# Windowed attention with a mixture of experts: all heads of q and k of six late groups loaded in 128 B runs by quarters of partitions and turned by VectorE, and the expert pieces of a step grouped two and two

## The chip, the cores and the metric

The kernel runs on one core of a Trainium2 chip. The metric is the device time of one execution in microseconds, the median of the runs. A core has TensorE (PE; its weight loads are shown as PEld), VectorE (DVE), ScalarE (ACT), GpSimd (POOL), and SyncE (SP), which here issues most transfers. Each engine works through its own instructions in a fixed order and waits on semaphores for the others; 16 DMA engines move the data.

## The reference

q, k and v are 8 batches × 8 heads × 576 positions × 64, all f32. Each position sees itself and the 63 before it. The attention's rows (4608 tokens of 512) then go through a layer of 8 experts, of which each token takes the one with the largest logit:

```python
rel = pos[:, None] - pos[None, :]
scores = np.where((rel >= 0) & (rel < 64), q @ k.T / 8, -1e9)
x = softmax(scores) @ v                      # heads side by side: (4608, 512)
logits = x @ w_gate + modality_bias[modality_id]
e = argmax(logits); gate = softmax(logits)[e]
out[rows of e] = gate * (relu(x[rows of e] @ w1[e]) @ w2[e])   # 512 -> 1024 -> 512
```

## The kernel before

**Attention.** The sequence is cut into 72 blocks of 64 positions, two blocks to a step `s` (36 steps, then four that drain), two steps to a group `G` of four blocks. Step `s` issues, in this order: `values` (the product with v) and `logits` for earlier steps, `scores(s)`, `minima(s)` on VectorE, `probs_t(s - 1)` (the probabilities turned by TensorE), `exps` on ScalarE, and `x_t(s - 2)`, the turning of the attention's finished rows, which logits of the next step reads. A step also prepares half of the next group's q and k: step 2G - 2 turns the heads of k of group G, step 2G - 1 those of q, in two parts of four heads each (`PARTS`). `heads_t` makes four TensorE transposes of 128 × 128 against an identity, two heads of even or odd positions in each; `heads_out` copies the result out of PSUM into `kT` or `qT` (VectorE; ScalarE for the second half of k). In the second step of a group `route2` ranks the tokens of an earlier group R by expert (three small matmuls, the "ranks"), `route3` and VectorE turn the ranks into addresses (`cnt`, `tgt`), and `scatter` writes the rows to a scratch in memory, sorted by expert.

**PSUM.** From step FIRST = 12 on, `turn_bank` gives the logits, the probabilities, the rows, the ranks and the q and k parts a bank each in turn out of a pool of two (`tp`). A part waits until the bank two turns back has been read.

**Experts.** From step 12 on the two most frequent experts already work, on slots of 256 rows out of the scratch. A slot is cut into 16 pieces of TensorE work of equal size (`first`: w1, lines L304; `second`: w2, L326; each product in three matmuls of high and low parts, so a hidden tile is split by ScalarE, `hh`, and VectorE, `hl`). `gap(it, True)` issues one piece; steps 12 and later have four such gaps, one behind the probabilities, one behind the rows, one behind each q or k part. Pieces that read hh and hl stand two pieces behind those that made them. When the attention is over, the rest of the slots run back to back.

**Loads.** `at` is a table from steps to loads, and a step issues its loads first, all on SP's queue: v of the step, k of group G in step 2G - 3 and q in step 2G - 2 (one step earlier for groups 1 to 7). Two `qk` buffers serve k and q in turns. SP also issues the weights (`y`, in `weights`) and the slots' rows (`xt`); it issues strictly in order, so one that waits holds up those behind it. Routing operations wait in a list (`routing`) that `tick` empties a few at a time; `run_later` issues what the last piece left for VectorE and ScalarE.

Of the kernel before, what the change touches and what calls it, by code (L numbers as in the profile page):

```python
# [8 lines left out]
F32 = mybir.dt.float32  # L9
# [17 lines left out]
def tile_window_attn_moe(  # L27
# [101 lines left out]
    def tick(n=1, table=False):  # L129
        for _ in range(n):  # L130
            if routing and not table:
                routing.pop(0)()
            elif queue:
                queue.pop(0)()
                issued[0] += 1
# [111 lines left out]
    def run_later():  # L247
        while later:
            later.pop(0)()
# [212 lines left out]
    def gap(it, wait=False):  # L462

        if next(it, "end") != "end" and not wait:
            run_later()
            tick()
# [40 lines left out]

    PARTS = ((K0, K1), (Q0, Q1))
    AHEAD = range(1, 8)
    WARM = 8, 3  # L510

    n_tp = [0]

    def turn_bank(s):

        i = n_tp[0]
        n_tp[0] += 1
        if s < FIRST and i % 5 > 1:
            return ps_m.tile([P, 512], F32, name=("em", "y0", "y1")[i % 5 - 2])
        return ps_t.tile([P, 512], F32, name="tp")  # L520
# [28 lines left out]
        else:  # L549
            qk[G, nm] = work.tile([P, 2, H, D], F32, name="qk", bufs=2)  # L550

    def load_qk(G, nm, blocks=range(GBLK), dma=nc.sync):

        t = qk[G, nm]
        x = q if nm == "q" else k
        i = blocks[0]
        while i <= blocks[-1]:
            b, g = divmod(GBLK * G + i, BPB)
            n = min(BPB - g, blocks[-1] + 1 - i)
            src = x[b, :, g * W64:(g + n) * W64].rearrange("h (p t) d -> p t h d", t=2)  # L560
            p0 = i * W64 // 2
            for par in range(2):
                dma.dma_start(out=t[p0:p0 + n * W64 // 2, par], in_=src[:, par])
            i += n

# [118 lines left out]
    def x_t(p, xp):  # L684
        xa = st[p, "xa"]
        for c in range(NC1):
            turn(xp[:, c * P:(c + 1) * P], xa[:, c * P:(c + 1) * P])
        xaT = st[p, "xT"] = work.tile([P, DM], F32, name="xaT")
        nc.scalar.copy(out=xaT, in_=xp)
# [13 lines left out]
            out=st[G, "lg"][:, j, :], in0=lt[:, 0:E], in1=bias_sel[:, p, :], op=ALU.add)  # L703

    chosen = {0: first_oh}

    def route1(G):

# [40 lines left out]
    def route3(G, rk):  # L749

        ex, oh = st.pop((G, "r")), chosen.pop(G)
        xg = [st.pop((GB * G + j, "xa")) for j in range(GB)]
        tgt = small.tile(sh3, F32, name="tgt")
        nc.vector.tensor_tensor(
            out=tgt, in0=rk.rearrange("p (j e) -> p j e", e=E), in1=ebase, op=ALU.add)
        se = small.tile([P, GB], F32, name="se")
        dst = small.tile([P, GB], F32, name="dst")
        idx = small.tile([P, GB], I32, name="idx")
        routing.append(lambda: nc.vector.reduce_sum(out=se, in_=ex, axis=AX.X))
        routing.append(lambda: nc.vector.tensor_tensor(out=tgt, in0=tgt, in1=oh[:, 1:], op=ALU.mult))  # L760
        routing.append(lambda: nc.vector.tensor_scalar(
            out=se, in0=se, scalar1=1e-9, scalar2=None, op0=ALU.add))
        routing.append(lambda: nc.vector.reduce_sum(out=dst, in_=tgt, axis=AX.X))

        def gates():
            for j in range(GB):
                nc.vector.reciprocal(out=xg[j][:, DM:DM + 1], in_=se[:, j:j + 1])
        routing.append(gates)

        def scatter(j):  # L770
            p = GB * G + j
            nc.gpsimd.tensor_copy(out=xg[j][:, DM + 1:DM + 2], in_=idc[:, p:p + 1])
            ins = nc.gpsimd.indirect_dma_start(  # L773
                out=xs, out_offset=bass.IndirectOffsetOnAxis(ap=idx[:, j:j + 1], axis=0),
                in_=xg[j], in_offset=None)
            tc.declare_no_dep(ins.ins, group="scatter", reason="rows are distinct")
            tc.add_to_no_dep_group("scatter", ins.ins)
            late = [T for T, _ in EARLY if T < G]
            if late:
                tc.declare_no_dep(ins.ins, group="early_loads", reason="rows read are older")  # L780
            for T in late:
                tc.add_to_no_dep_group(f"scatter_after_{T}", ins.ins)

        def rows():
            nc.vector.tensor_copy(out=idx, in_=dst)
            for j in range(GB):
                scatter(j)
            scattered.append(f"scatter_after_{G}")
        routing.append(rows)

    def counts(G, tp):
        cp = tp[:, GB * E:E + GB * E]
# [55 lines left out]
    def when(step, f, *args):  # L848
        at.setdefault(max(step, -1), []).append((f, args))
# [9 lines left out]
    for G in range(1, NG):  # L859
        ahead = 1 if G in AHEAD else 0  # L860
        for nm, step in (("k", 2 * G - 3 - ahead), ("q", 2 * G - 2 - ahead)):
            when(step, new_qk, G, nm)
            when(step, load_qk, G, nm)

    pieces = []
    raws = []
# [155 lines left out]

    for s in range(NPR + 4):
        j = s % GB
        for f, args in at.pop(s, ()):
            f(*args)
        n_tick = 6 if s < FIRST else 5
        n_gap = 0 if s < FIRST else 4
        G = s // GB + 1
        heads = PARTS[j] if G < NG else ()  # L1030
        R = (s - 5) // GB if s >= 5 and j == 1 else -1
        if 1 <= s < FIRST:
            swap_upper(s - 1)

        if 2 <= s < NPR + 2:
            values(s - 2)
            if s <= FIRST:
                values_out(s - 2)
        if 3 <= s < NPR + 3:
            logits(s - 3, turn_bank(s) if s != FIRST else ps_m.tile([P, 512], F32, name="y0"))  # L1040
            if (s - 3) % GB == GB - 1:
                route1((s - 3) // GB)
        if FIRST < s < NPR + 2:
            values_out(s - 2)
        if s < NPR:
            scores(s)
            if s == FIRST:
                x_turn(fetched[0])
                gap(it, True)
            minima(s)  # L1050
            if s == FIRST - 2:
                tick(todo[0][-1] - issued[0], table=True)
        if 1 <= s <= NPR:
            if s == FIRST:
                run_later()
            if s >= FIRST:
                swap_upper(s - 1)
            swap_v(s - 1)
            for a in range(2):
                probs_t(s - 1, a, turn_bank(s))  # L1060
            sums(s - 1)
        if s < NPR:
            exps(s, (0, 1))
        if s == 0:
            first_pair(1, (both[:1], both[1:]))
            cast_bias()
        if n_gap > 0 and s != FIRST:
            gap(it, True)
        if 2 <= s < NPR + 2:
            x_t(s - 2, turn_bank(s) if s != FIRST else ps_m.tile([P, 512], F32, name="y0"))  # L1070
        run_later()
        tick(2)
        if s < NPR:
            exps(s, (2, 3, 4))
        if n_gap > 0:
            if FIRST < s < FIRST + 4 or s % 2:
                weights(s)
            if s != FIRST:
                gap(it, True)
        if heads:  # L1080
            tp = turn_bank(s)
            heads_t(G, *heads[0], tp)
            heads_out(tp, G, *heads[0], nc.vector.tensor_copy)
        if s == FIRST:
            weights(s)
            gap(it, True)
        run_later()
        tick(n_tick)
        cnt = None
        if R >= 0:  # L1090
            tp = turn_bank(s)
            rk = route2(R, tp)
            if R == NG - 1 or any(R == T for T, _ in EARLY):
                cnt = counts_out(tab if R == NG - 1 else pl, counts(R, tp))
            route3(R, rk)
        if s < NPR:
            exps(s, (5, 6, 7))
        if n_gap > 2:
            if FIRST <= s < FIRST + 4:
                weights(s)  # L1100
            gap(it, True)
        if heads:
            tp = turn_bank(s)
            heads_t(G, *heads[1], tp)
            heads_out(tp, G, *heads[1], nc.scalar.copy if heads[1] == K1 else nc.vector.tensor_copy)
        run_later()
        tick(n_tick)
        if s == WEIGHTS:
            load_weights()
        if s >= WEIGHTS:  # L1110
            weights(s)
        if n_gap > 3:
            gap(it, True)
        run_later()
        if s == 1:
            select_bias()
        if s == 4:
            nc.sync.dma_start(out=xs_blk[DUMMY:DUMMY + 2].rearrange("b p c -> p b c"), in_=padrow)
        for T, xs_ in EARLY:
            if T == R:  # L1120
                plan(T, xs_, cnt)
    tick(len(routing))
    tick(len(queue))


# [266 lines left out]
```

## Time and profile before

| | |
|---|---|
| median of the runs | 622.13 us (621.25 to 622.3, three runs) |
| the profiled execution | 621.29 us, of which the program's span is 619.6 us |
| TensorE busy | 603.5 us |
| VectorE, ScalarE, GpSimd busy | 381.8, 297.4, 139.7 us |
| moved by DMA | 88.08 MB in 158983 packets |

Engine times are the union of an engine's instructions. TensorE's matmuls overlap one another, so the duration of one says less than the distance from its start to the start of the next. "Idle before" is time in which an engine stood still, with what ended it. Lines L are those of the kernel before.

### The profile page before, as it was taken

Reading aid. Unit: us, or ns where it says so; the run is one execution under the profiler, and the core shown is the slowest. Engines: PE = TensorE matmul, PEld = TensorE weight load, DVE = VectorE, ACT = ScalarE, POOL = GpSimd, SP = SyncE. Lnnn points to the kernel's source line nnn. Section 1 sums busy time; section 2 is a strip of 40 time slices with the busy share of each in tenths; the row PEclk is TensorE's granted clock in tenths of the full one; section 3 lists DMA queues with packets and bytes.
Section 4 is the critical chain, followed back from the end, with each engine's and each line's share of the span. In section 5 each row is a group of like instructions: output and inputs, shape, how many; then the busy total and the mean of one; then the engine's idle time right before and its main releaser. Section 6 shows DMA issues by size and latency. Waiting matters only on the chain. (4 is left out here: it accounts for less than half of the span.)

```text
span 619.6 us, 17314 instructions
## 1 busy us (share of the span) xinstructions
PE 603.5 (97%) x6365; PEld 542.2 (88%) x6365; DVE 381.8 (62%) x1486; ACT 297.4 (48%) x933; POOL 139.7 (23%) x315
## 2 busy tenths in 40 slices
PE   8999889999999999999999999999999999999996
PEld 5888778889898998989898899999999989999986
DVE  3899987877776877667656465323324734776622
ACT  3999886765757555636463111111112513554411
POOL 6333422042313320321223131011001101102202
PEclk7999999999999999999999999999999999999999
DMA  9999865764675754463313034522243534678300
GB/s 163 216 234 246 204 183 166 188 188 126 167 205 123 194 135 99 137 155 84 107 54 103 35 103 167 174 69 69 51 155 116 167 126 137 203 239 249 108 18 21
DMA packets 158983, 88.08 MB, mean 142 GB/s; under 512 B 122618, under 2 KB 141616, under 8 KB 158768
## 3 DMA queue, kind: packets, MB, share of 16 engines
q1 hardware_dynamic: 150272, 67.45, 43.1%
q0 software_dynamic: 5888, 18.93, 8.1%
q8 instruction: 51, 0.84, 0.6%
q10 hardware_dynamic: 2736, 0.58, 0.5%
q14 instruction: 36, 0.29, 0.2%
HBM read 67.49 MB, written 23.91 MB: 148 GB/s over the span
## 5 line engine op out<-in xcount | busy, mean ns | idle before, releaser
L326 PE MATMUL y<-Whi,hh 128*128 128x512 f32 x288 | 116.9, 406 | 0.0
L638 ACT ACTIVATE ss<-ss,mn 128x128 f32<-128x128 f32 x288 | 112.6, 398 | 4.0 <-DMA wg<-in_moe_w_gate_dram 3.3
L326 PE MATMUL y<-Wlo,hh 128*128 128x512 f32 x288 | 112.7, 391 | 0.0
L326 PE MATMUL y<-Whi,hl 128*128 128x512 f32 x288 | 112.5, 391 | 0.0
L337 POOL DMA_INDIRECT out_dram<-y,id x36 | 39.8, 1107 | 232.7 <-DVE y L334 159.9
L313 DVE SCALAR_TENSOR_TENSOR hl<-em,hh 128x512 fp32r<-128x512 f32 x50 | 34.5, 690 | 92.8 <-ACT hh L312 82.1
L304 PE MATMUL em<-xh,Whi 128*128 128x256 f32 x400 | 83.7, 290 | 0.0
L312 ACT ACTIVATE hh<-em 128x512 fp32r<-128x512 f32 x50 | 29.6, 592 | 105.2 <-PE em L304 86.9
L304 PE MATMUL em<-xl,Whi 128*128 128x256 f32 x400 | 79.3, 280 | 0.0
L304 PE MATMUL em<-xh,Wlo 128*128 128x256 f32 x400 | 79.1, 279 | 0.0
L647 ACT COPY pT<-tp 128x512 f32<-128x512 f32 x57 | 31.4, 589 | 70.2 <-PE tp L470 60.9
L626 DVE CUSTOM_DVE_ANT_0 ss<-sp,masks 128x128 f32<-128x128 f32 x288 | 63.5, 286 | 2.4 <-PE sp L612 2.3
L326 PEld LDWEIGHTS y<-Whi,hl 128*128 128x128 f32 x288 | 54.1, 188 | 12.2
L304 PEld LDWEIGHTS em<-xh,Whi 128*128 128x128 f32 x400 | 62.3, 189 | 1.8
L326 PEld LDWEIGHTS y<-Whi,hh 128*128 128x128 f32 x288 | 54.2, 188 | 8.2
L326 PEld LDWEIGHTS y<-Wlo,hh 128*128 128x128 f32 x288 | 54.2, 188 | 7.9
L304 PEld LDWEIGHTS em<-xl,Whi 128*128 128x128 f32 x400 | 60.9, 188 | 0.0
L304 PEld LDWEIGHTS em<-xh,Wlo 128*128 128x128 f32 x400 | 60.9, 188 | 0.0
L638 ACT ACTIVATION_READ_ACCUMULATOR ss<-ss,mn 128x1 f32 x288 | 56.0, 195 | 0.0
L773 POOL DMA_INDIRECT xs_scratch<-xa,idx x36 | 36.4, 1012 | 81.8 <-DVE lm L716 40.3
L312 ACT ACTIVATE hh<-sp 128x512 fp32r<-128x512 f32 x22 | 13.2, 598 | 75.9 <-PE sp L304 73.9
L668 PEld LDWEIGHTS av<-ve,pT 128*64 128x64 f32 x576 | 36.3, 138 | 13.2 <-issue 8.2
(240 smaller groups left out, 1211.3 us busy)
## 6 DMA issues: line engine op xcount, KB each, us to landing
xt<-xs_scratch SPq DMA_DIRECT2D x72, 128.0 KB
vo<-in_v_dram SPq DMA_DIRECT2D x32, 256.0 KB
y<-in_moe_w_dram SPq DMA_DIRECT2D x32, 256.0 KB
vo<-in_moe_w_dram SPq DMA_DIRECT2D x24, 256.0 KB
ss<-in_moe_w_dram SPq DMA_DIRECT2D x24, 256.0 KB
xs_scratch<-xs_scratch SPq DMA_DIRECT2D x8, 514.0 KB
pT<-in_moe_w_dram SPq DMA_DIRECT2D x16, 256.0 KB
qk<-in_k_dram SPq DMA_DIRECT2D x14, 256.0 KB
```

The costliest lines, as they stand in the source:

```text
L304: nc.tensor.matmul(out=hb[:, i * TP:(i + 1) * TP], lhsT=w[buf][:, c0:c0 + P], rhs=x[:, c * TP:(c + 1) * TP], start=(n == 0), stop=(n == le ...
L312: nc.scalar.activation(out=hh, in_=hb, func=AF.Relu),
L313: nc.vector.scalar_tensor_tensor(out=hl, in0=hb, scalar=0.0, in1=hh.bitcast(F32), op0=ALU.max, op1=ALU.subtract)))
L326: nc.tensor.matmul(out=sl["y", t], lhsT=h[:, i * TP + t * P:i * TP + (t + 1) * P], rhs=w[buf][:, c0:c0 + DM], start=(k == 0 and n == 0), s ...
L337: ins = nc.gpsimd.indirect_dma_start(out=out, out_offset=bass.IndirectOffsetOnAxis(ap=sl["id"][:, t:t + 1], axis=0), in_=y, in_offset=None ...
L626: nc.vector.tensor_tensor_reduce(out=ss[a][:, hp, :], in0=sp[a][:, hp * P:(hp + 1) * P], in1=mask, scale=-1.0 / 8.0, scalar=3.0e38, op0=AL ...
L638: nc.scalar.activation(out=ss[a][:, hp, :], in_=ss[a][:, hp, :], func=AF.Exp, bias=mn[:, h:h + 1], scale=-1.0, accum_out=sm[:, h:h + 1])
L647: nc.scalar.copy(out=pT, in_=pp)
L668: nc.tensor.matmul(out=by_block(av)[c * W64:(c + 1) * W64, a, :, hp, :], lhsT=pT[:, i:i + W64], rhs=(vo if c else ve)[p][:, 2 * hp + a, :] ...
L773: ins = nc.gpsimd.indirect_dma_start(out=xs, out_offset=bass.IndirectOffsetOnAxis(ap=idx[:, j:j + 1], axis=0), in_=xg[j], in_offset=None)
```

## The change

**Quartered loads and VectorE's turns.** For a group of G ≥ 9 whose four blocks lie in one batch (groups 9, 10, 12, 14, 16 and 17), q and k are no longer loaded with positions on partitions in runs of 256 B. A load puts each half head (32 of 64 numbers, 128 B) of 32 positions on one of the four quarters of the partitions, one DMA to a quarter of a head: 16 DMAs of 32 partitions to a tensor. Laid out so, the 32 × 32 blocks that a VectorE transpose turns are those that `kT` and `qT` want, and one transpose of 128 × 512 out of the load's tile (`turn_heads`) takes the place of four TensorE transposes and the copy. Behind step 12 a step's loads are no longer issued first but in lots: the values and the first two heads behind the first piece, two heads behind the rows' place, two behind the second part, the rest at the end (`loads`).

**The order of a step behind 12.** The four pieces stand in pairs: two, then the ranks (in the second step of a group), the rows' transposes and the first q or k part, then one piece, the second part, one piece. In quartered groups there are no TensorE transposes in the parts, so the pieces follow two and two. ScalarE and VectorE get the same order: the copy of the turned rows, xaT, behind the third to fifth exponential, and cnt and tgt ahead of the first q part.

**Scatters.** From group HOLD = 4 on, a group's last routing entry (the addresses' cast and the scatters) is held until the next step's first piece is due (`release`), which first empties the routing list.

On TensorE, step 19 (the second step of group 10); ss are the probabilities, xa the rows, qk the heads, em and y the pieces' products, tri and ones the ranks. Before:

```order
L470 MATMUL tp<-ident_r,ss 128x128 x8
L304 MATMUL em<-xh,Whi_65 128x256 x2
...
L470 MATMUL tp<-ident_r,xa_103 128x128 x4
L304 MATMUL em<-xh,Wlo_66 128x256 x2
...
L470 MATMUL tp<-ident_r,qk 128x128 x4
L740 LDWEIGHTS tri
L740 MATMUL tp<-oh,tri 128x16
...
L326 MATMUL y_2877<-Whi_65,hh 128x512
...
L470 MATMUL tp<-ident_r,qk 128x128 x4
L326 MATMUL y_2900<-Whi_65,hh 128x512
```

Step 19 now:

```order
L470 MATMUL tp<-ident_r,ss 128x128 x8
L304 MATMUL em<-xh,Whi_65 128x256 x2
...
L771 LDWEIGHTS tri
L771 MATMUL tp<-oh,tri 128x16
...
L470 MATMUL tp<-ident_r,xa_103 128x128 x4
L326 MATMUL y_2902<-Whi_65,hh 128x512
...
L326 MATMUL y_2922<-Whi_65,hh 128x512
```

Both qk blocks are gone, and two pieces stand on either side of the ranks and the rows.

On VectorE, step 21 (the second step of group 11, which is not quartered), from the copy of v's upper half on. Before:

```order
L542 COPY ve<-vo 64x512
L119 TENSOR_TENSOR Wlo_67<-y,Whi_2499 128x512
L577 COPY qT<-tp 128x2x2x128
L313 SCALAR_TENSOR_TENSOR hl<-em,hh 128x512
L798 COPY cnt<-tp 1x8
L754 TENSOR_TENSOR tgt<-tp,ebase 128x16
```

Now:

```order
L543 COPY ve<-vo 64x512
L119 TENSOR_TENSOR Wlo_67<-y,Whi_2511 128x512
L829 COPY cnt<-tp 1x8
L785 TENSOR_TENSOR tgt<-tp,ebase 128x16
L600 COPY qT<-tp 128x2x2x128
L313 SCALAR_TENSOR_TENSOR hl<-em,hh 128x512
```

cnt and tgt, which read the ranks' bank, have moved ahead of the copy of q and of hl.

On SP, the loads of group 10 (steps 17 and 18); vo is v, y a piece of a weight. Before:

```order
L528 DMA vo<-in_v_dram 128x8x64
L563 DMA qk<-in_k_dram 128x8x64 x2
L107 ISA
L107 DMA y<-in_moe_w_dram 128x512
L103 ISA
L103 DMA y<-in_moe_w_dram 128x512
L528 DMA vo<-in_v_dram 128x8x64
L563 DMA qk<-in_q_dram 128x8x64 x2
```

Now:

```order
L529 DMA vo<-in_v_dram 128x8x64
L582 DMA qk<-in_k_dram 32x8x32 x12
L103 ISA
L103 DMA y<-in_moe_w_dram 128x512
L582 DMA qk<-in_k_dram 32x8x32 x4
L529 DMA vo<-in_v_dram 128x8x64
L582 DMA qk<-in_q_dram 32x8x32 x12
```

Two DMAs of 128 partitions have become 16 of 32, the last four behind a weight's load.

The core of the diff:

```diff
+    QUARTERS = 9
+    def quartered(G):
+        return G >= QUARTERS and GBLK * G // BPB == (GBLK * G + GBLK - 1) // BPB
+    def by_heads(t):
+        return t.rearrange("p t h d -> p (t h d)").rearrange("p (h u d) -> p h u d", h=HP, d=R32)
+    def turn_heads(G, nm, i):
+        dst = by_group(qT if nm == "q" else kT)[:, G % 2, 2 * i:2 * i + 2]
+        nc.vector.transpose(
+            out=dst.rearrange("p h j i -> p (h j i)"),
+            in_=by_heads(qk[G, nm])[:, 2 * i:2 * i + 2].rearrange("p h u d -> p (h u d)"))
...
+            for h in turned:
+                for c in range(2):
+                    rows = slice((h % 2 * 2 + c) * R32, (h % 2 * 2 + c + 1) * R32)
+                    src = x[b, h, g * W64:(g + n) * W64, c * R32:(c + 1) * R32]
+                    dma.dma_start(out=by_heads(t)[rows, h // 2, u, :],
+                                  in_=src.rearrange("(u p) d -> p u d", p=R32))
...
+    held = []
+    HOLD = (FIRST + 1 - 5) // GB
+    def release():
+        if held:
+            tick(len(routing))
+            held.pop(0)()
...
-        routing.append(rows)
+        (held if G >= HOLD else routing).append(rows)
...
-            when(step, load_qk, G, nm)
+            for h in range(0, H if quartered(G) else 1, 2):
+                turned = range(h, h + 2) if quartered(G) else range(0)
+                when(step, load_qk, G, nm, range(GBLK), nc.sync, turned)
...
+            release()
             gap(it, True)
+            run_later()
+            tick(2)
+            if s < NPR:
+                exps(s, (2, 3, 4))
+            if s < FIRST + 4 or s % 2:
+                weights(s)
+            loads(3)
+            gap(it, True)
+            cnt = ranks()
+            if s < NPR + 2:
+                x_t(s - 2, turn_bank(s))
+            part(0)
+            run_later()
+            tick(n_tick)
+            loads(1)
+            if s < NPR:
+                exps(s, (5, 6, 7))
         if n_gap > 2:
...
+        part(1)
         run_later()
         tick(n_tick)
+        if s > FIRST:
+            loads(1)
```

`part(i)` calls `turn_heads` in a quartered group and `heads_t` and `heads_out` in the others; `ranks` holds what stood in line. Steps up to 12 keep their order.

More of the change, by code (lines that the diff above doesn't have):

```diff
@@ L550, in new_qk, with load_qk @@
             qk[G, nm] = work.tile([P, 2, H, D], F32, name="qk", bufs=2)
-    def load_qk(G, nm, blocks=range(GBLK), dma=nc.sync):
+    def quartered(G):
[7 more added lines that the diff above has]
+            in_=by_heads(qk[G, nm])[:, 2 * i:2 * i + 2].rearrange("p h u d -> p (h u d)"))
+    def load_qk(G, nm, blocks=range(GBLK), dma=nc.sync, turned=range(0)):
         t = qk[G, nm]
@@ L559, in load_qk @@
             n = min(BPB - g, blocks[-1] + 1 - i)
-            src = x[b, :, g * W64:(g + n) * W64].rearrange("h (p t) d -> p t h d", t=2)
             p0 = i * W64 // 2
-            for par in range(2):
+            u = slice(i * W64 // R32, (i + n) * W64 // R32)
+            for h in turned:
[4 more added lines that the diff above has]
+                                  in_=src.rearrange("(u p) d -> p u d", p=R32))
+            for par in range(0 if turned else 2):
+                src = x[b, :, g * W64:(g + n) * W64].rearrange("h (p t) d -> p t h d", t=2)
                 dma.dma_start(out=t[p0:p0 + n * W64 // 2, par], in_=src[:, par])
@@ L1024, in tile_window_attn_moe @@
         j = s % GB
-        for f, args in at.pop(s, ()):
-            f(*args)
+        if s <= FIRST:
+            for f, args in at.pop(s, ()):
+                f(*args)
         n_tick = 6 if s < FIRST else 5
@@ L1031, in tile_window_attn_moe, with loads, part, ranks @@
         R = (s - 5) // GB if s >= 5 and j == 1 else -1
+        def loads(n):
+            for f, args in at.get(s, [])[:n]:
+                f(*args)
+            at[s] = at.get(s, [])[n:]
+        def part(i):
+            if not heads:
+                return
+            if quartered(G):
+                turn_heads(G, *heads[i])
+                return
+            tp = turn_bank(s)
+            heads_t(G, *heads[i], tp)
+            heads_out(tp, G, *heads[i], nc.scalar.copy if heads[i] == K1 else nc.vector.tensor_copy)
+        def ranks():
+            if R < 0:
+                return None
+            tp = turn_bank(s)
+            rk = route2(R, tp)
+            n = None
+            if R == NG - 1 or any(R == T for T, _ in EARLY):
+                n = counts_out(tab if R == NG - 1 else pl, counts(R, tp))
+            route3(R, rk)
+            return n
         if 1 <= s < FIRST:
@@ L1066, in tile_window_attn_moe @@
             cast_bias()
-        if n_gap > 0 and s != FIRST:
-            gap(it, True)
[L1069 to L1076, printed above, removed]
-                weights(s)
[L1078 to L1085, printed above, removed]
-            gap(it, True)
[L1087 to L1097, printed above, removed]
+        if s <= FIRST:
+            if s >= 2:
+                x_t(s - 2, turn_bank(s) if s != FIRST else ps_m.tile([P, 512], F32, name="y0"))
+            run_later()
[3 more added lines that the diff above has]
+            part(0)
+            if s == FIRST:
+                weights(s)
[4 more added lines that the diff above has]
+            exps(s, (5, 6, 7))
+        else:
+            release()
+            gap(it, True)
+            run_later()
+            tick(2)
+            if s < NPR:
+                exps(s, (2, 3, 4))
+            if s < FIRST + 4 or s % 2:
+                weights(s)
+            loads(3)
+            gap(it, True)
+            cnt = ranks()
+            if s < NPR + 2:
+                x_t(s - 2, turn_bank(s))
+            part(0)
+            run_later()
+            tick(n_tick)
+            loads(1)
+            if s < NPR:
+                exps(s, (5, 6, 7))
         if n_gap > 2:
@@ L1101, in tile_window_attn_moe @@
             gap(it, True)
[L1102 to L1105, printed above, removed]
+        part(1)
         run_later()
         tick(n_tick)
+        if s > FIRST:
+            loads(1)
         if s == WEIGHTS:
@@ L1111, in tile_window_attn_moe @@
             weights(s)
+        if s > FIRST:
+            loads(9)
         if n_gap > 3:
@@ L1122, in tile_window_attn_moe @@
     tick(len(routing))
+    release()
     tick(len(queue))
```

## The prediction

> **What bounds the kernel now.** I read the page first, then the busy times by stretch, then TensorE's own timeline inside one step, then the timelines of VectorE and of SP's queue.
>
> ```profile
> span 619.6 us, 17314 instructions
> ...
> PE 603.5 (97%) x6365; PEld 542.2 (88%) x6365; DVE 381.8 (62%) x1486; ACT 297.4 (48%) x933; POOL 139.7 (23%) x315
> ```
>
> TensorE is busy for 97% of the span. That alone is weak, since matmuls overlap, so I ask where it idles:
>
> ```profile
> 100.00:150.00 50.00, 49.32 (x633) 44.09 (x633) 36.87 (x159) 33.30 (x114) 14.31 (x27) 1.00 0.61 168
> 150.00:200.00 50.00, 50.00 (x647) 45.36 (x646) 37.10 (x165) 32.04 (x112) 11.88 (x25) 1.00 0.62 160
> 200.00:250.00 50.00, 50.00 (x667) 44.82 (x666) 38.22 (x182) 29.09 (x102) 11.53 (x26) 1.00 0.56 139
> 250.00:300.00 50.00, 50.00 (x673) 45.12 (x673) 33.25 (x160) 26.87 (x101) 15.17 (x30) 1.00 0.48 128
> ```
>
> The columns are the length, then busy PE, PEld, DVE, ACT and POOL, the granted clock, the DMA engines' share, GB/s. The clock is full. Between 150 and 300 us TensorE has no idle time at all; before that, 0.68 us in 50. Steps 13 to 33, which the change rewrites, lie in these rows. No other engine is above 38.2 of 50. What is taken from TensorE here shortens the run; what is put on the others costs nothing until one of them is waited for. One step on TensorE (step 24):
>
> ```profile
> 203.08 1.10 PE L612 MATMUL sp<-kT,qT 64*64 64x128 f32 x32
> ...
> 204.97 0.48 PE L326 MATMUL y<-Whi,hh 128*128 128x512 f32 x1
> 205.28 0.39 PE L326 MATMUL y<-Wlo,hh 128*128 128x512 f32 x1
> 205.51 0.40 PE L326 MATMUL y<-Whi,hl 128*128 128x512 f32 x1
> ...
> 206.44 0.60 PE L470 MATMUL tp<-ident_r,xa 128*128 128x128 f32 x4
> 206.79 0.48 PE L304 MATMUL em<-xh,Whi 128*128 128x256 f32 x2
> 207.12 0.40 PE L304 MATMUL em<-xh,Wlo 128*128 128x256 f32 x2
> ...
> 208.28 0.60 PE L470 MATMUL tp<-ident_r,qk 128*128 128x128 f32 x4
> 208.64 0.48 PE L304 MATMUL em<-xh,Whi 128*128 128x256 f32 x2
> 208.96 0.40 PE L304 MATMUL em<-xh,Wlo 128*128 128x256 f32 x2
> ...
> 210.12 0.60 PE L470 MATMUL tp<-ident_r,qk 128*128 128x128 f32 x4
> 210.48 0.47 PE L326 MATMUL y<-Whi,hh 128*128 128x512 f32 x1
> 210.80 0.39 PE L326 MATMUL y<-Wlo,hh 128*128 128x512 f32 x1
> ...
> 213.55 1.10 PE L612 MATMUL sp<-kT,qT 64*64 64x128 f32 x32
> ```
>
> Read starts, not durations: the step takes 10.47 us, and each instruction follows the one before without a hole. A block of four transposes holds TensorE for 0.35 to 0.36 us (206.44 to 206.79, 208.28 to 208.64, 210.12 to 210.48). The first matmul behind transposes takes 0.31 to 0.33 us to the next one, where inside a piece it is 0.23 (205.28 to 205.51): each return from transposes to a piece costs about 0.09 us.
>
> **The change, part by part.** *Removed from TensorE.* In six groups (9, 10, 12, 14, 16, 17) each of two steps loses two blocks: 24 × 0.355 = 8.5 us, all on the path.
>
> *Regrouped.* A step had four returns to a piece (behind the probabilities, the rows and two blocks of q or k). A quartered step keeps two, so 12 × 2 = 24 go; the nine other steps of 13 to 33 run the rows' transposes and the first q or k block back to back and lose one each. 33 × 0.09 = 3.0 us. Bounds: 0 if a merged pair pays it inside, 3.3 at 0.10; I take 3.0, since the four returns above agree. Steps 34 to 37 keep their two.
>
> *A new wait on a PSUM bank.* In the second step of a group the ranks' matmuls now stand directly ahead of the rows' transposes. The bank pool turns over two banks, so in an unquartered group the next q block needs the ranks' bank back, which VectorE frees by cnt and tgt. Step 21 of before, TensorE and then VectorE:
>
> ```profile
> 176.54 0.60 PE L470 MATMUL tp<-ident_r,qk 128*128 128x128 f32 x4
> 176.98 0.17 PE L740 MATMUL tp<-oh,tri 128*128 128x16 bf16 x1
> ...
> 177.05 0.17 PE L793 MATMUL tp<-oh,ones 128*128 128x8 bf16 x1
> ```
>
> ```profile
> 175.41 0.69 DVE L119 TENSOR_TENSOR Wlo<-y,Whi 128x512 fp32r<-128x512 f32 x1
> 177.18 0.69 DVE L577 COPY qT<-tp 128x512 f32<-128x512 f32 x1 [1.07 <-PE tp L470]
> 178.16 0.69 DVE L313 SCALAR_TENSOR_TENSOR hl<-em,hh 128x512 fp32r<-128x512 f32 x1 [0.29 <-ACT hh L312]
> 178.77 0.14 DVE L798 COPY cnt<-tp 1x8 f32<-1x8 f32 x1
> 178.84 0.15 DVE L754 TENSOR_TENSOR tgt<-tp,ebase 128x16 f32<-128x16 f32 x1
> ```
>
> VectorE was done with Wlo at 176.10 and idled 1.07 us; cnt came late only because qT and hl stood ahead of it. Now cnt and tgt stand ahead of both. From the end of the ranks to the end of tgt is then about 0.3 to 0.5 us, and the rows' block covers 0.355 of it: 0.15 us in each of five steps (13, 15, 21, 25, 29), 0.7 us. Behind the waiting block on TensorE stand the third and fourth piece, so it is time lost to the end. Bounds: 0 (a wait added ahead of TensorE's work brings no gain), and 1.6 each, the distance from the end of L793 to cnt above.
>
> *Moved to VectorE.*
>
> ```profile
> L577 DVE COPY qT<-tp 128x512 f32<-128x512 f32 x27 | 18.5, 687 | 17.9 <-PE tp L470 17.7
> L577 ACT COPY kT<-tp 128x512 f32<-128x512 f32 x15 | 9.2, 613 | 0.0
> L266 DVE STREAM_TRANSPOSE xt<-xt 128x512 f32<-128x512 f32 x37 | 24.0, 687 | 1.0 <-DMA xt<-xs_scratch 0.9
> ```
>
> A turn of 128x512 f32 costs 0.687 us (L266), what the copy that it replaces cost. 24 turns replace 18 copies on VectorE and 6 on ScalarE: VectorE gains 6 × 0.687 = 4.1 us, ScalarE loses 3.7. Its cover: TensorE needs the turned heads only in the next group's scores, a step later. In the fullest step,
>
> ```profile
> 192.40:203.00 10.60, 10.60 (x144) 9.57 (x142) 8.53 (x38) 7.41 (x24) 1.26 (x5) 1.00 0.73 172
> ```
>
> VectorE works 8.53 of 10.6 us; that step shrinks to some 9.7 and gets no turn more than it loses copies. A turn waits for the DMAs of its four heads; behind it on VectorE stand hl, which TensorE reads two pieces later, and the step's last small operations, then the next step's minima. If the cover were gone and VectorE a microsecond late, those two pieces (some 2.8 us) would absorb it. 0. The same holds for xaT, which moves behind three exponentials on ScalarE: its reader, the next step's logits, is two pieces and the values away. 0.
>
> *Loads.* Per group and tensor 16 DMAs of 32 KB replace two of 256 KB (or four), in four lots within the step. Queued behind them on SP are the values, weights and rows.
>
> ```profile
> 196.10 3.57 SPq L563 DMA_DIRECT2D qk<-in_k_dram  x4
> ...
> 223.31 2.50 SPq L211 DMA_DIRECT2D xt<-xs_scratch  x5
> ```
>
> ```profile
> 242.54 1.96 SPq L563 DMA_DIRECT2D qk<-in_q_dram  x4
> 248.85 0.39 SPq L528 DMA_DIRECT2D vo<-in_v_dram  x1
> ...
> 253.00 1.07 SPq L563 DMA_DIRECT2D qk<-in_k_dram  x2
> ```
>
> One issue costs 0.49 (242.54), 0.50 (223.31; these too write 32 partitions), 0.54 (253.00) or, held up, 0.89 us (196.10). I take 0.49, the same tensor on the same queue: 7.8 us for 16, plus 0.4 for the values, in a step of 9.7. It fits, with about a step from a load's lots to their turns. At 0.89 it would be 14.6. On the DMA engines:
>
> ```profile
> q1 hardware_dynamic: 150272, 67.45, 43.1%
> ...
> q10 hardware_dynamic: 2736, 0.58, 0.5%
> ```
>
> q10 gives 0.005 × 16 × 619.6 us / 2736 = 18 ns a packet. A load goes from 2048 packets of 256 B to 4096 of 128 B: from 2.3 us of all engines to between 2.3 (by bytes) and 4.6 us (by packets). I take 4.6: 0.24 of a step more, on shares of 0.48 to 0.62. Covered.
>
> The Trainium skill speaks against this part: its page "DMA: Bandwidth & Descriptors", section Specifications, asks for at least 512 B per transfer and has the engine read, modify and write below that; no run here shows 128 B. If that doubled a packet, see rival three.
>
> *Scatters held* to the next step's head: the same POOL instructions, POOL under 16 of 50 us busy, and VectorE's small routing operations ahead of them come before that step's first hl, which has two pieces' time. 0.
>
> Sum: −8.5 − 3.0 + 0.7 = −10.8 us. The profiled execution took 621.3 us, so 610.5; it lies 0.8 below the median of the runs (622.1), and against that I forecast 611.3.
>
> **The rivals.**
> One, the bank: if VectorE is as late with cnt as above, five steps wait 1.6 us: 622.1 − 11.5 + 8 = 618.6. Against it: its 1.07 us of idling. Chance 0.05.
>
> Two, slower: SP's queue. If an issue costs 0.89 us throughout, a quartered step's 14.6 us fall 4.9 us behind its 9.7. A run of such steps starts with a step less the last lot's four issues, 9.7 − 2.0, about 8 us of slack. The two runs of four steps (groups 9 and 10, 16 and 17) then lose 19.6 − 8 = 11.6 us each, the two of two steps 1.8 each: 27 us reach VectorE's turns, then the scores: 622.1 − 11.5 + 27 = 638. It decides against the change where two runs of four lose 11.5 us, (11.5 + 16)/8 = 3.4 us a step, 0.80 us an issue. For it: 3.57 us above; against it: that load waited for its buffer, and 1.96. Slower 0.04; partly late, 613 to 620, 0.08.
>
> Three, the packets: at 36 ns a load takes 9.3 us of all engines, 7.0 more, 0.72 of a step on shares near 0.6: 0.3 × 9.7 = 2.9 us too much per step. A run of four then loses 11.6 − 8 = 3.6 us, one of two nothing: 622.1 − 11.5 + 7 = 618. Against it: the packets of q10 (580 kB in 2736, 212 B on average) took 18 ns, while the average q1 packet, of 449 B (67.45 MB in 150272), took 0.431 × 16 × 619.6 / 150272, 28 ns: the time follows the bytes, not a step below 512. The skill's rule above would give this. Chance 0.02.
>
> Four, larger.
>
> ```profile
> L470 PE MATMUL tp<-ident_r,qk 128*128 128x128 f32 (+1 forms) x176 | 25.6, 271 | 0.9 <-DMA qk<-in_k_dram 0.9
> ```
>
> If a transpose were worth its own duration, 0.271 us, 96 would give 26 us: 596. Against it: four start within 0.36 us. "TensorE: Matmul & The Clock Gate" of the Trainium skill, Part 4, gives about 275 ns for one; the trace agrees on the duration, not on what it holds. Chance 0.02.
>
> Five: the freed time fills with other waits and nothing moves, 622; against it the idle time of all others. Chance 0.03.
>
> **How the numbers follow.** My case has 0.76: 608 (11.8 saved, the 0.68 us of idling gone too, 0.3% of scatter between runs) to 616 (8.5 saved, 2.5 lost). With the lower half of the partly late case the range holds 0.80; the bank, the packets and the larger gain lie outside. Faster by over 0.2% (about what a measurement of this kernel tells from no change): 0.76 + 0.05 + 0.08 + 0.02 + 0.02 = 0.93; within 0.2% 0.03; slower 0.04.
>
> **What would show it.** Right: TensorE's busy time falls by some 11 us, still no idling from 150 to 300 us; quartered steps take 9.6 to 9.8 us, unquartered ones 10.4 to 10.6; 24 turns of 0.69 us. Wrong: TensorE idles before a q block behind ranks (bank), VectorE idles before a turn for a DMA and then TensorE before scores (queue), or packets of 128 B take over 18 ns.

## The result, and the profile after

The changed kernel took 629.14 us (median of 6 runs, 625.94 to 631.66) against 622.21 of the kernel before: a ratio of 1.0116, 95% interval 1.0094 to 1.0138. Forecast were 611.3 us, range 608 to 616; so the change is slower where it was to be faster. The page of the profiled execution, the slowest of the six (span 629.9 us, the kernel before 619.6), its busy times and one of its groups:

```profile
span 629.9 us, 17357 instructions
...
PE 598.6 (95%) x6269; PEld 534.4 (85%) x6269; DVE 389.5 (62%) x1492; ACT 295.2 (47%) x927; POOL 142.8 (23%) x315
...
L635 PE MATMUL sp<-kT,qT 64*64 64x128 f32 x1152 | 42.9, 288 | 12.0 <-DVE qT L564 11.3
```

TensorE issues 96 instructions fewer, as announced, and its busy time falls by only 4.9 us; 12.0 us of idling have come in ahead of the scores (L635), 11.3 of it for VectorE's qT. Where, the busy times by stretch say (length, PE, PEld, DVE, ACT, POOL, granted clock, DMA share, GB/s):

```profile
100.00:150.00 50.00, 48.85 (x635) 43.43 (x637) 39.48 (x172) 33.46 (x116) 14.54 (x25) 1.00 0.63 156
150.00:200.00 50.00, 42.22 (x529) 36.99 (x522) 33.63 (x143) 26.39 (x91) 13.40 (x24) 0.93 0.61 145
200.00:250.00 50.00, 45.23 (x587) 39.65 (x586) 34.99 (x158) 25.36 (x89) 11.33 (x22) 0.93 0.60 139
250.00:300.00 50.00, 50.00 (x667) 44.55 (x666) 36.86 (x172) 29.35 (x107) 12.04 (x27) 1.00 0.58 127
```

Where the kernel before had no idle time from 150 to 300 us, 7.8 and 4.8 us are now idle in two stretches, and the clock there is 0.93. From 250 us on TensorE is busy throughout. A quartered step did become as short as forecast; TensorE in step 18 and at the head of step 19:

```profile
140.22 1.10 PE L635 MATMUL sp<-kT,qT 64*64 64x128 f32 x32
...
149.76 1.10 PE L635 MATMUL sp<-kT,qT 64*64 64x128 f32 x32
...
152.18 0.66 PE L470 MATMUL tp<-ident_r,ss 128*128 128x128 f32 x4 [0.73 <-ACT pT L670]
```

From scores to scores 9.54 us, 10.48 before. The last row is a small new loss: the second half of the probabilities' transposes waits for ScalarE's copy of the first half, apparently because both halves got the same PSUM bank here (so in steps 17, 19 and 33, 0.9 us each over back-to-back issue).

The long wait lies at step 20. TensorE, VectorE and SP's queue there, and SP's queue of the kernel before at the same place:

```profile
168.01 1.13 PE L635 MATMUL sp<-kT,qT 64*64 64x128 f32 x16 [6.96 <-DVE qT L564]
```

```profile
165.47 1.30 DVE L266 STREAM_TRANSPOSE xt<-xt 128x512 f32<-128x512 f32 x2 [6.62 <-DMA xt<-xs_scratch]
...
167.25 0.71 DVE L564 STREAM_TRANSPOSE qT<-qk 128x512 f32<-128x512 f32 x1
```

```profile
156.47 0.36 SPq L103 DMA_DIRECT2D y<-in_moe_w_dram  x1
156.88 1.91 SPq L582 DMA_DIRECT2D qk<-in_q_dram  x4
159.73 3.77 SPq L211 DMA_DIRECT2D xt<-xs_scratch  x5
```

```profile
150.39 2.71 SPq L211 DMA_DIRECT2D xt<-xs_scratch  x5
```

Read it backwards. TensorE waits 6.96 us for the turn of q. VectorE had been idle for 6.62 us, not for q's loads but for a slot's rows (xt), whose turn stands ahead of q's. SP issued those rows at 159.73, behind the last of q's sixteen loads; before the change they went out at 150.39. A second such wait, 4.38 us at 215.00, has the same two steps (VectorE idle for xt, 4.77 us). Behind the wait the clock:

```profile
163.00:168.00 5.00, 0.00 (x0) 0.00 (x0) 2.53 (x10) 1.14 (x2) 0.43 (x3) 0.69 0.74 170
168.00:170.00 2.00, 1.99 (x20) 1.44 (x20) 2.00 (x3) 0.00 (x0) 1.86 (x3) 0.50 0.88 184
170.00:172.00 2.00, 1.91 (x8) 1.58 (x8) 1.97 (x13) 1.15 (x3) 0.20 (x1) 0.56 0.96 262
172.00:174.00 2.00, 2.00 (x15) 1.83 (x14) 1.85 (x13) 1.11 (x7) 0.00 (x0) 1.00 1.04 234
```

For four microseconds after the wait TensorE works at half clock, which costs another 2 us: step 20 took 19.56 us, 9.1 more than in the kernel before, of which 6.96 are the wait. "TensorE: Matmul & The Clock Gate" of the Trainium skill, Part 1, says that TensorE falls to half clock after an idle window of about 3.4 us and needs about 3.4 us of work to come back. These rows agree; in e3 below, a shorter wait was enough.

### The profile page after: what moved, and what is told of

It reads as the page before. It is cut to its first block, busy times and chain, and to the rows that moved or that the text cites. A ratio compares the mean times of both kernels' runs of the same rounds, so it can differ in the third digit from the quotient of the medians.

```text
span 629.9 us, 17357 instructions
## 1 busy us (share of the span) xinstructions
PE 598.6 (95%) x6269; PEld 534.4 (85%) x6269; DVE 389.5 (62%) x1492; ACT 295.2 (47%) x927; POOL 142.8 (23%) x315
## 4 chain that ended last, share of the span: by engine, by line
PE 73%; DVE 4%; SPq 3%; ACT 3%; DMA 2%; issue 2%; POOL 0%; POOLq 0%; DVEq 0%; ACTq 0%
PE y L326 28%; PE em L304 20%; PE sp L304 10%; PE tp L470 6%; PE av L691 3%; PE sp L635 3%; SPq L582 2%; PE tp L720 1%; ACT ss L661 1%; PE y L377 1%; DVE xl L196 1%; DVE xt L266 1%; DMA qk<-in_k_dram 1%; DMA xt<-xs_scratch 1%; DMA vo<-in_v_dram 1%
## 5 line engine op out<-in xcount | busy, mean ns | idle before, releaser
L304 PE MATMUL em<-xh,Whi 128*128 128x256 f32 x400 | 81.7, 285 | 0.0
L635 PE MATMUL sp<-kT,qT 64*64 64x128 f32 x1152 | 42.9, 288 | 12.0 <-DVE qT L564 11.3
```

Source lines behind the costliest of these rows:

```text
L304: nc.tensor.matmul(out=hb[:, i * TP:(i + 1) * TP], lhsT=w[buf][:, c0:c0 + P], rhs=x[:, c * TP:(c + 1) * TP], start=(n == 0), stop=(n == le ...
L635: nc.tensor.matmul(out=sp[a][c * W64:(c + 1) * W64, hp * P:(hp + 1) * P], lhsT=qT[rows, place(g + c, hp), :], rhs=kT[rows, win(c, hp), :], ...
```

## The experiments

Ratios are to the kernel before, run on the same chip.

**One edit each on the changed kernel, and its parts.** *e1, rows ahead:*

```diff
+                    if k == 2 and i == 0 and nxt is None:
+                        nxt = fetch()
+                        turn_at = 1
```

> The changed kernel with one edit: a slot's rows are fetched three pieces earlier, so that on SP's queue their five loads stand ahead of q's sixteen instead of behind them. Theory (the rows' load waits its turn on SP's queue, VectorE waits for it, and the turn of q behind it makes TensorE wait before the scores): both long waits of TensorE, 6.96 us at 168 and 4.38 us at 215, go, and with them the slow clock behind each, about 2 us apiece; 629 - 11.3 - 4 = 614 us, if q's last lots, now 2.5 to 3.8 us later, do not take their place; 614 to 620. Rival one (VectorE has too much to do with the turns): the waits stay, 626 to 631. Rival two (the regrouped order of pieces is what costs): no change, 626 to 631.

650.37 us, 1.0471 [1.0434, 1.0508]: far worse. The rows now come before q's loads; VectorE's turns wait for these, and TensorE for the turns (elsewhere ScalarE waits for a weight, 7.88 us at 113.32):

```profile
166.68 0.71 DVE L567 STREAM_TRANSPOSE qT<-qk 128x512 f32<-128x512 f32 x1 [4.76 <-DMA qk<-in_q_dram]
171.77 0.71 DVE L567 STREAM_TRANSPOSE qT<-qk 128x512 f32<-128x512 f32 x1 [2.09 <-DMA qk<-in_q_dram]
```

The wait has changed its victim. It has also grown: SP stood still for 5.5 us (151.2 to 156.6) ahead of the rows, most of it because they could not be read before scatters had landed in the scratch. So e1 changed more than the order. *e2, loads ahead of weights:*

```diff
+            loads(9)
             if s < FIRST + 4 or s % 2:
                 weights(s)
-            loads(3)
```

> The changed kernel with one edit: all loads of a step are issued ahead of its weights' loads instead of between and behind them. Theory: SP's queue no longer holds lots behind a weight whose buffer is still read (4.1 us at 130.6 in the changed kernel); the queue gains about 4 us before the rows of the first long wait, which shrinks from 7 to about 3 us: 623 to 626 us. If the queue is simply full of issues, it gains nothing: 628 to 631. Rival (VectorE or the regrouping): no change, 626 to 631.

637.74 us, 1.0262 [1.0237, 1.0286], worse again. Now the weight is last, behind k's sixteen. ScalarE, which splits it, stands in front of it, the copy of the probabilities behind that, and TensorE (126.62, 7.51 us) behind the copy:

```profile
124.42 0.62 ACT L114 CAST Whi<-y 128x512 fp32r<-128x512 f32 x1 [9.27 <-DMA y<-in_moe_w_dram]
```

Three orders of the same queue, three victims: rows, q, weight. Both expectations took the order for the fault; none of the three had room for all its issues in time. *e3, no quartered group* (`QUARTERS = 99`):

> The changed kernel without quartered groups (the bound is set at group 99): only the pairs of pieces, the ranks' and rows' new place, the loads' place and the held scatters are left. The prediction's price for this part is 9 x 0.09 + 12 x 0.09 saved less some 1.2 us of waits on the ranks' bank: 621. My reading of the changed kernel now: a merged pair of transposes holds TensorE as long as two apart (0.79 us against 0.71 + 0.09), and unquartered steps there take 0.1 to 0.2 us more than before, so 21 x 0.1 to 0.2 = 2 to 4 us more: 624 to 626. Rival (the regrouping makes the long waits): 630 or more.

627.51 us, 1.0088 [1.0061, 1.0116]. More than either price. One wait, in step 25, on TensorE, on VectorE and on GpSimd:

```profile
218.84 0.78 PE L470 MATMUL tp<-ident_r,ss 128*128 128x128 f32 x4 [2.69 <-DVE lg L725]
```

```profile
217.96 0.75 DVE L334 TENSOR_SCALAR y<-y,gate 128x512 f32<-128x512 f32 x1 [4.02 <-DMA out_dram<-y,id]
```

```profile
209.85 1.06 POOL L804 DMA_INDIRECT xs_scratch<-xa,idx  x1 [8.34 <-DVE e_n_p L154]
...
211.39 0.97 POOL L804 DMA_INDIRECT xs_scratch<-xa,idx  x1 [0.28 <-issue]
...
212.66 1.00 POOL L337 DMA_INDIRECT out_dram<-y,id  x1 [0.21 <-issue]
```

VectorE may not write the next output tile (y) until an earlier one has left, and that write stood on GpSimd behind the two held scatters. *e4, only groups 14, 16 and 17* (`QUARTERS = 14`):

> The changed kernel with only groups 14, 16 and 17 quartered, whose loads meet no weights on SP's queue. Theory: no long wait, since q's loads and the rows' there were done in time in the changed kernel too; six steps save 0.93 us each, 5.6 us in all, against the regrouping alone (624 to 626): 618 to 621. Rival (128 B packets, or the turns on VectorE, cost everywhere): no better than the regrouping alone, 624 to 628.

627.38 us, 1.0104 [1.0071, 1.0137]: the saving of six steps is not to be seen. TensorE lost 2.3 us at the scores of two steps with "issue", no releaser, while four indirect DMAs of GpSimd stood back to back.

**The held scatters taken back.** Edit in f1 and f2: `HOLD = NG`, that is, none is held; f2 has `QUARTERS = 14` besides.

> The changed kernel with one edit: no scatters are held (the bound is set at the last group), so they stand in the routing list as before. Theory as it now stands, in two parts: in the changed kernel the long waits come from the slot's rows late on SP's queue, so they stay here, 626 to 630; the held scatters are what costs in the two kernels without early quartered groups. Rival (the held scatters make the long waits, by what they put on GpSimd's queue ahead of the output's writes): the two long waits shrink, 612 to 618.

625.83 us, 1.0054 [1.0030, 1.0077]: the two long waits stay, as the theory said, but they shrink (the scores wait 3.7 and 2.7 us instead of 6.96 and 4.38), so the held scatters had a part in them, as the rival said.

> Groups 14, 16 and 17 quartered, no scatters held. In the run with the same groups and held scatters TensorE lost 2.3 us with nothing that the profile names while four indirect DMAs of GpSimd (two scatters, two writes of the output) stood back to back, and 2 us more by the slow clock behind it; in the regrouped kernel VectorE waited 4.02 us for a write of the output that stood behind two held scatters. Theory (the held scatters did that): both go, 622.1 - 5.6 + 1 to 2 for the regrouping = 617 to 619. Rival (these waits come from the turns' loads or from the regrouped pieces): no change against the held ones, 625 to 629.

616.99 us, 0.9916 [0.9893, 0.9939]: as the theory said, 10 us better than with held scatters, and faster than the kernel before. TensorE by stretch:

```profile
100.00:150.00 50.00, 49.96 (x664) 44.37 (x663) 37.41 (x159) 31.78 (x109) 12.02 (x24) 1.00 0.63 166
150.00:200.00 50.00, 50.00 (x611) 44.85 (x609) 37.50 (x171) 33.09 (x115) 11.27 (x22) 1.00 0.66 167
200.00:250.00 50.00, 50.00 (x669) 45.19 (x669) 39.31 (x182) 29.73 (x110) 16.41 (x32) 1.00 0.61 149
250.00:300.00 50.00, 49.27 (x659) 43.91 (x659) 36.06 (x174) 27.59 (x102) 13.36 (x26) 1.00 0.58 123
```

**Quartering alone, in the order of before.** f3 is the kernel before with the six groups quartered, loads at a step's head; f4 the same with groups 14, 16 and 17:

```diff
-        if heads:
+        if heads and quartered(G):
+            turn_heads(G, *heads[0])
+        elif heads:
             tp = turn_bank(s)
```

> The kernel before with all six groups quartered and nothing else: the order of a step, the scatters and the place of the loads (at a step's head) are those of before. TensorE saves 24 x 0.355 + 24 x 0.09 = 10.7 us. Theory (the rows' load stands behind q's sixteen issues on SP's queue): the two long waits come here too, 7 + 4.4 us and some 4 us of slow clock: 622.1 - 10.7 + 15 = 626, 620 to 630. Rival (regrouping or held scatters make the long waits): 611 to 614.

622.99 us, 1.0012 [0.9998, 1.0027]. A wait comes here without any regrouping, though on the weight, as in e2, not on the rows: ScalarE 8.69 us at 123.85, TensorE 7.07 us at 126.05.

> The kernel before with groups 14, 16 and 17 alone quartered, nothing else changed. Theory: their loads meet no weights on SP's queue, nothing waits, and six steps save 0.89 us each: 622.1 - 5.3 = 616.8, 615.5 to 618. Rival (the saving on TensorE comes back elsewhere whatever the order): 621 to 623.

617.65 us, 0.9927 [0.9904, 0.9949]: faster, as expected. So the three late groups gain 4.4 to 5.1 us in either order, and the three early ones lose: 625.83 - 616.99 = 8.8 us in the new order, 622.99 - 617.65 = 5.3 in the old, where their steps should have gained some 5.5.

**The issues alone.** g3 is the kernel before with the loads of groups 9, 10 and 12 cut into sixteen by heads; runs of 256 B, bytes, transposes and order stay:

```diff
+                if G in (9, 10, 12):
+                    for h in range(H):
+                        dma.dma_start(out=t[p0:p0 + n * W64 // 2, par, h], in_=src[:, par, h])
+                else:
```

> The kernel before with one edit: the loads of q and k of groups 9, 10 and 12 are cut into sixteen by heads, with the same 256 B runs, bytes, transposes and order. Nothing is gained, so this is the price of the issues alone. Theory (issues on SP's queue): the weight or the rows behind them come late as in the changed kernel, and TensorE waits: a step is longer here (10.5 instead of 9.6 us), so less is lost than there: 625 to 633. Rival (the 128 B packets or VectorE's turns are what is late): 621 to 623.

630.52 us, 1.0136 [1.0107, 1.0166]. With nothing else changed, more issues cost 8.1 us. SP's queue, ScalarE and TensorE there:

```profile
112.03 8.35 SPq L565 DMA_DIRECT2D qk<-in_k_dram  x16
120.63 1.52 SPq L103 DMA_DIRECT2D y<-in_moe_w_dram  x3
```

```profile
123.35 0.62 ACT L114 CAST Whi<-y 128x512 fp32r<-128x512 f32 x1 [8.25 <-DMA y<-in_moe_w_dram]
```

```profile
125.54 1.11 PE L470 MATMUL tp<-ident_r,ss 128*128 128x128 f32 x4 [6.63 <-ACT pT L651]
```

Sixteen issues, 8.35 us; the weight behind them; ScalarE; TensorE. It is the chain of f3 with neither a 128 B packet nor a turn of q or k in it. The opposite edit takes issues off SP and leaves bytes, packets and turns: f1 with a part of the loads of groups 9, 10 and 12 issued by ScalarE (g1 every fourth, `h % 2 and c`; g2 every second, `c`).

```diff
+                    q_ = nc.scalar if G < 14 and c else dma
-                    dma.dma_start(out=by_heads(t)[rows, h // 2, u, :],
+                    q_.dma_start(out=by_heads(t)[rows, h // 2, u, :],
```

> The changed kernel without held scatters (625.8 us) and with one more edit: in groups 9, 10 and 12 every fourth of the sixteen loads is issued by ScalarE instead of SP; bytes, packets and turns stay. Theory (SP's queue has too many issues while weights come): in steps 15 to 18 SP's 45.6 us of work shrinks by 16 x 0.53 to 37, under the 41 us of the four steps, and the rows come in time: the waits of 4 and 3 us with the clock behind them shrink by more than half: 614 to 621. Rival (the DMA engines or the 128 B packets are late, not the issues): no change, 624 to 628.

623.50 us, 1.0016 [1.0001, 1.0032]: a little better than f1 (1.0054), less than the theory asked; the rows still come late (2.58 us at the scores of step 20).

> As the run before it, but half of the loads of groups 9, 10 and 12 on ScalarE. Theory: SP is then free of the delay (8 issues a step), 612 to 617, unless ScalarE, which has some 3.8 us free in a step of 9.7, is held up by 8 issues of 0.45 us = 3.6 us: then TensorE waits for the copies of the probabilities, 618 to 626. Rival (the DMA engines or the packets): 624 to 628.

618.10 us, 0.9924 [0.9902, 0.9946]: 7.7 us better than f1. The rows go out at 151.57 and no wait of several microseconds is left:

```profile
151.57 2.45 SPq L211 DMA_DIRECT2D xt<-xs_scratch  x5
```

The same bytes in the same packets, so the DMA engines were not the limit; the number of issues on one queue was.

**The order of pieces, and the scatters' place.** g4 is e3 with no scatters held:

> The regrouped order alone, without quartered groups and without held scatters. Theory (a merged pair of transposes saves nothing, and the held scatters cost the 5 us of the regrouped kernel): 621.5 to 623.5. Rival (regrouping itself costs): 625 to 628. The prediction's price for it: 620 to 621.

627.85 us, 1.0086 [1.0064, 1.0108]: a miss, as slow as e3, though by another loss. Five steps (14, 18, 22, 30, 34) took 1.3 to 1.4 us longer than in f2, with two or three holes on TensorE at the scores, for nothing that the profile names; one of these steps, and GpSimd there:

```profile
183.60 0.46 PE L635 MATMUL sp<-kT,qT 64*64 64x128 f32 x4 [0.18 <-issue]
184.36 0.41 PE L635 MATMUL sp<-kT,qT 64*64 64x128 f32 x3 [0.30 <-issue]
185.11 0.97 PE L635 MATMUL sp<-kT,qT 64*64 64x128 f32 x25 [0.33 <-issue]
```

```profile
182.13 1.07 POOL L804 DMA_INDIRECT xs_scratch<-xa,idx  x1 [6.49 <-DVE Wlo L119]
...
183.68 0.97 POOL L804 DMA_INDIRECT xs_scratch<-xa,idx  x1 [0.28 <-issue]
```

Scatters at the scores, one might say. But f2 has the same order up to step 25, the same two scatters at 179.20 and 180.76, and its scores run through:

```profile
180.42 1.10 PE L635 MATMUL sp<-kT,qT 64*64 64x128 f32 x32
```

Two runs then moved the scatters. h1 is e3 with the release behind the first piece and what it leaves; h2 is g4 with the ranks behind the first q part again:

```diff
-            release()
             gap(it, True)
             run_later()
+            release()
```

> The regrouped order alone (no quartered groups), scatters held, but released behind the first piece instead of ahead of it, so that GpSimd issues an output write, two scatters, a write, as before the change. Theory (VectorE waited for a write that stood behind the two scatters): that wait goes, 622 to 624. Rival (the regrouped pieces themselves cost): 626 to 628.

622.62 us, 1.0013 [1.0001, 1.0024]. GpSimd's order is write, scatters, write again, both kinds of wait are gone, and 4.9 us with them (627.51 to 622.62):

```profile
207.47 1.05 POOL L337 DMA_INDIRECT out_dram<-y,id  x1 [7.39 <-DVE lg L748]
...
209.27 0.98 POOL L804 DMA_INDIRECT xs_scratch<-xa,idx  x1 [0.54 <-POOL xa L803]
...
210.73 0.98 POOL L804 DMA_INDIRECT xs_scratch<-xa,idx  x1 [0.28 <-POOL xa L803]
...
213.80 0.98 POOL L337 DMA_INDIRECT out_dram<-y,id  x1 [2.00 <-DVE rw L699]
```

> The regrouped order alone, scatters not held, and the ranks again behind the first q block. In the run without that last edit the scatters were issued around the step's end (138.6 and 140.2, the scores at 139.9) and TensorE lost some 1.2 us at the scores of five steps with no releaser named. Theory (the scatters at the scores do it): with the ranks later the scatters move into the step, the gaps go, 621.5 to 623.5. Rival (the place of the ranks and scatters has nothing to do with it): 626 to 628.

625.41 us, 1.0047 [1.0030, 1.0064]: a miss by 2 us. The holes at the scores are gone, but the ranks now wait for a bank (0.29 us for ScalarE's copy of the rows in step 17), and the second steps of groups take 11.1 us instead of 10.7.

The last two join the cures: h3 is g2 with held scatters released as in h1, h4 is e4 with that release.

> All six groups quartered, half of the loads of groups 9, 10 and 12 on ScalarE, scatters held and released behind the first piece. Theory (issues on SP, and the scatters' place, are all that kept the saving back): 12 quartered steps save 0.9 us each, 622.2 - 10.8 + 2 for the copies of the probabilities that share a bank and for ScalarE's issues: 612 to 615. Rival (ScalarE's issues hold TensorE up in the early groups): no better than the same with scatters not held, 617 to 619.

617.90 us, 0.9937 [0.9920, 0.9953]: a miss, no better than g2, as the rival said. What is left are smaller waits in the early groups, as in step 20:

```profile
160.55 0.67 PE L636 MATMUL sp<-kT,qT 64*64 64x128 f32 x16 [0.85 <-DVE qT L564]
162.40 0.65 PE L470 MATMUL tp<-ident_r,ss 128*128 128x128 f32 x4 [0.60 <-DVE lg L726]
```

> Groups 14, 16 and 17 quartered, scatters held and released behind the first piece. Theory: as without held scatters (617.0) or a little better, 615.5 to 617.5. Rival (holding costs by itself, wherever released): 624 to 628 as with the release ahead of the piece.

618.32 us, 0.9937 [0.9921, 0.9954]: nearly as expected, against 1.0104 with the early release. The best measured are f2 (616.99) and f4 (617.65), which are not told apart by their intervals; f4 is the smaller change.

## Why the prediction was wrong, point by point

**Removed from TensorE, 8.5 us: right.** A quartered step without waits took 9.54 to 9.72 us, 10.47 or 10.65 before. Three groups, six steps, gave 4.4 us in f4 and 5.1 in f2, of which this term makes 12 x 0.355 = 4.3. TensorE's busy time fell by 4.9 us instead of some 11, as work at half clock counts double; in g2, without the long waits, it fell by 9.3 (to 594.2). The 275 ns of rival four stand in "TensorE: Matmul & The Clock Gate" of the Trainium skill, Part 4, beside a bf16 transpose; those here are f32, so that the trace has the same duration confirms little.

**Loads, "It fits": this is the step that failed.** The sum was 7.8 us of issues plus 0.4 for the values in a step of 9.7. The price of one was right:

```profile
L582 SPq DMA_DIRECT2D qk<-in_k_dram x96: 312/449/1517, 114.4 to 299.0; - x96
```

The columns after the count are the shortest, the median and the longest issue in ns; their mean is 0.51 us, and sixteen in a row take 8.35 us (g3) to 9.72 (the changed kernel at 235.86). What the sum left out stands in the same queue: a weight or two to a step, the five issues of a slot's rows (3.77 us at 159.73), and a few long issues (eleven of the 192 took 1.0 to 1.7 us). From 113.8 to 163.5 us SP's issues, with the short instructions between them, took about 45.6 us, for four steps of some 41, and SP stood still another four (131.0 to 134.9) before a weight whose buffer an output write was still reading. That write stood on GpSimd behind two held scatters, of which the second is shown:

```profile
128.02 0.97 POOL L804 DMA_INDIRECT xs_scratch<-xa,idx  x1 [0.28 <-POOL xa L803]
...
129.29 1.22 POOL L337 DMA_INDIRECT out_dram<-y,id  x1 [0.22 <-DVE hl L313]
```

In f1, with none held, it went out at 125.03, SP did not stand there, and the scores of step 20 waited 3.65 us instead of 6.96. After the weights (from step 25) the same sixteen fit, and groups 14, 16 and 17 had no long wait.

**Rival two (SP's queue, slower) was the mechanism, at 0.04.** Its turning point, 0.80 us an issue, was worked out with an empty queue but for the values; with the weights and rows in it, 0.52 was enough. And its victim was wrong: it sent the lateness to the turns through their own loads. Which load is late depends on the order: rows in the changed kernel, q in e1, a weight in e2, f3 and g3. Since VectorE and ScalarE work in order, each led to TensorE. The text counted one cover (hl, two pieces away) and not that a slot's rows are turned on the same engine ahead of q.

**Scatters held, 0: failed.** Priced by engine time; what it changed was GpSimd's order. Held and released ahead of the piece, two scatters stand ahead of an output write that VectorE, or SP's next weight, needs gone; e3 to h1 it is 5 us. From e4 to h4 it is 9 us, most of it in the two steps with holes at the scores, whose cause is not shown. In the changed kernel itself 3.3 (f1), by way of SP as above.

**Regrouped, -3.0, and the bank, +0.7.** The mechanism of the bank fits (in step 29 the first q block starts 0.63 us behind the rows' block, 0.43 without ranks ahead, and right behind tgt), the regrouping's saving was mis-sized: h1 (1.0013) is no faster than the kernel before, f2 and f4 are alike. A merged pair, step 28:

```profile
262.94 0.60 PE L470 MATMUL tp<-ident_r,xa 128*128 128x128 f32 x4
263.37 0.60 PE L470 MATMUL tp<-ident_r,qk 128*128 128x128 f32 x4
263.73 0.48 PE L304 MATMUL em<-xh,Whi 128*128 128x256 f32 x2
```

263.73 - 262.94 = 0.79 us, against 0.71 for two blocks apart: the pair pays inside what it saves behind. That was the lower bound of the text, 0 for the nine unquartered steps. In quartered ones two returns vanish with the blocks in any order (f4).

**The stall's size.** Nothing in the text priced a slow clock behind a wait; it adds some 2 us to each.

**Rival three (packets) is refuted.** 128 B packets did not take 36 ns. The after page:

```profile
q1 hardware_dynamic: 177536, 67.46, 44.5%
```

0.445 x 16 x 629.9 us is 212 us more than q1 took before, with 24576 packets of 256 B (18 ns, as q10) replaced by 49152 of 128 B: (442 + 212) / 49152 = 13 ns each at most. The rule of "DMA: Bandwidth & Descriptors" of the Trainium skill, Specifications, that the engine reads, modifies and writes below 512 B, does not show as a doubled time here.

**What stays open.** Why TensorE's scores have holes in g4 and e4 and not in f2 was not settled: scatters or writes of GpSimd are near in each case, but the same scatters near the same scores did nothing in f2. Why the second half of the probabilities waited for the first in three steps was not tried either. And no run brought home the some 5.5 us that the early groups should save: the best with all six quartered (h3, 617.90) is no faster than the late three alone (f4, 617.65).

## What to carry to other kernels

A queue that issues in order is an engine with a capacity: before loads are cut into more of them, add up every issue of the fullest steps, the other tensors' and the waits for buffers too, and compare with the step; a price per issue alone says nothing. When a queue is over-full, changing its order only picks who waits, and on in-order engines that waiter holds up work that has its data already. A step that is "moved, not added" is priced by what now stands behind it on its queue.

## What the runs showed of the hardware

Cutting a load into eight times as many, same packets, cost a queue 0.52 us each and the kernel 8.1 us (g3). A wait of TensorE of 2.69 us (e3) was already enough for a slow clock behind it:

```profile
219.00:221.00 2.00, 2.00 (x12) 2.00 (x12) 2.00 (x14) 1.28 (x6) 1.85 (x4) 0.56 0.23 90
221.00:223.00 2.00, 2.00 (x12) 2.00 (x12) 1.54 (x6) 1.75 (x8) 0.60 (x1) 0.59 0.11 41
```

A VectorE turn of 128x512 of q or k took 0.70 to 0.71 us, as forecast.
